# A routed two-layer network on Trainium2: the token list's comparisons and streamed columns laid out by column

## The chip, the cores and the metric

One core of a Trainium2 chip runs the whole program in one launch. The metric is the device time of one execution in microseconds (us); three executions of the kernel before took 3925.69, 3928.92 and 3929.18 us, median 3928.92.

The core's engines work side by side and wait for each other by semaphores: TensorE (PE; its weight loads are shown apart as PEld), VectorE (DVE), ScalarE (ACT), GpSimd (POOL) and the queues that issue transfers (SyncE and GpSimd here). In a matrix product one operand, the stationary one, is loaded as weights, and the columns of the other, the moving one, are streamed past it.

## The reference

```
X   = real(fft(fft(x, axis=1), axis=2))        # x: 8 x 3072 x 256
x   = X as 24576 rows of 256
# routing, capacity 3072 tokens for each of 8 experts, one expert per token
logits = x @ w_gate                            # 24576 x 8
for (token, e) in descending order of logits:
    if token is free and expert e has room: assign it
for e in experts:                              # 256 -> 1024 -> 256
    y[mask_e] = relu(x[mask_e] @ w1[e]) @ w2[e]
h   = y @ w_in                                 # 256 -> 2048
out = (max(h, 0) + alpha * min(h, 0)) @ w_out  # 2048 -> 256, float32
```

The greedy order is computed as eight rounds. In each round the expert that fills next gets its 3072 tokens, and the round's list of those tokens is formed; the list says which rows the expert's tiles gather.

## The kernel before, in words

**Stages.** `fft_phase` computes the transform, writes the rows to memory and leaves the logits in `LG`, token m of column c at partition m, column c (128 partitions, 192 columns). Then `ffn_phase` runs the first round alone, as all else waits for it, and after it 48 tiles of 512 tokens, six for each expert. The other seven rounds run as a generator, `background()`: the tile loop calls it once after each group of products (`l1` to `l4`), before that group's evacuation, and each call emits a small step of a round. Round r begins when tile 6(r − 2) is reached; where a tile's gather needs a list that is not formed yet, the loop draws the rest of the round's steps at once. The order of all instructions is the order in which the program emits them (a manual schedule); each engine takes its own in that order.

**A tile's products.** `l1` (tile `h`), `l2` (`y`), `l3` (`u`) and `l4` (`o`) are products of three parts each, and ScalarE and VectorE evacuate them: `hs`, and for `u` the operations `r`, `a`, `g`.

**A round's list.** `place` ends with `lh`, two 16-bit numbers for each token: its position among the chosen, low seven bits (`lh[:, 0]`) and the rest (`lh[:, 1]`, 0 to 23 for the chosen). The list is a product over partitions: for each of the 192 columns, the stationary operand `ol` (128 x 128) is 1 where a token's low number equals the output partition, and the moving operand `rr` (2 x 24 = 48 columns) holds the partition number and the column number where the token's high number equals the group (`eq`). 192 such products sum into `ls`, which becomes the list `lm` and the row numbers `idx`.

**pack_wide (L607 to L631)** is this for the first round: 24 comparisons on VectorE, one for each group over all 192 columns (L617); two ScalarE products with the partition number `pf` (L618); the products with the column number `colb` on GpSimd and VectorE (L620); then twelve times an `ol` of 16 columns (L625), 16 products (L627) and two dummy products (`warm`, L1028). Ahead of all stand 26 dummy products.

**pack (L633 to L657)** is this for the background rounds, in chunks of 8 columns: `eq` (L644), `ol` (L645) and the two halves of `rr` (L646, L647) on VectorE for two chunks, a pause of two steps (`lag`), then the 16 products (L653). There are 24 chunks in each of seven rounds.

In both, `eq` and `rr` have the group ahead of the column, so that the 48 elements streamed for one column lie apart:

```
rr = wp.tile([P, 2, NG, C], BF16, tag="rr", bufs=2, name="rr")    # pack, C = 8
lv, ol[:, :, j], rr[:, :, :, j]                                   # out, stationary, moving
```

**Beside the first round.** After each step of `pack_wide` the caller places a chunk of the first expert's weights (`place_w`: a ScalarE cast at L814, a GpSimd subtraction at L815) and fetches another (L837, GpSimd's queue). After the list come the gathers of the first rows (L886), 14 dummy products and the first tile.

Of the kernel before, what the change touches and what calls it, by code (L numbers as in the profile page):

```python
# [12 lines left out]
BF16 = mybir.dt.bfloat16  # L13
# [22 lines left out]
def fft_phase(tc, op, x, cWA, cCS, cT, wg, w3, XD, LG, W3S, router):  # L36
    """x -> rows of Re(FFT2) in XD (row = col*128 + m) and gate logits in LG[m, col, e];
    on the side the float64 weights w3 -> float32 halves in W3S."""
    nc = tc.nc
    with ExitStack() as ctx:  # L40
# [11 lines left out]
        def load_x(b, k, n=4):  # L52
            """n of the chunk's four columns, the last of them when part is there."""
            if (b, k) not in xch:
                xch[b, k] = xp.tile([N1, 4, D], F32, tag="x", name=f"x_{b}_{k}")
                o = 0
            else:
                o = 4 - n
            nc.sync.dma_start(
                xch[b, k][:, o : o + n], x[b].rearrange("(a c) d -> a c d", c=N2)[:, 4 * k + o : 4 * k + o + n, :]  # L60
            )
# [8 lines left out]
        # twiddled DFT-32 factors: for the cosine and the sine part, leading bits and rest  # L70
# [4 lines left out]
        def convert():  # L75
            """float64 words -> float32, rounded, as its leading 12 bits and the rest."""
# [13 lines left out]
            for n, (j, q) in enumerate(chunks):  # L90
                load(n + 1)
                raw = raws.pop(n)
                lo, hi = raw[:, :, 0], raw[:, :, 1]
                a = vp.tile([P, CV], I32, tag="a", bufs=1, name=f"a{n}")
                b = vp.tile([P, CV], I32, tag="b", bufs=1, name=f"b{n}")
                V.tensor_scalar(a, hi, 5, 2, op0=ALU.logical_shift_left, op1=ALU.logical_shift_right)
                V.tensor_scalar(b, lo, 28, 1, op0=ALU.logical_shift_right, op1=ALU.bitwise_and)
                yield
                V.scalar_tensor_tensor(a, lo, 29, a, op0=ALU.logical_shift_right, op1=ALU.bitwise_or)
                yield  # L100
                V.scalar_tensor_tensor(a, hi, -(1 << 30), a, op0=ALU.bitwise_and, op1=ALU.bitwise_or)
                yield
                V.tensor_tensor(a, a, b, op=ALU.add)
                # below float32's normal range: zero
                V.tensor_scalar(b, hi, 1, 21, op0=ALU.logical_shift_left, op1=ALU.logical_shift_right)
                yield
                f = b.bitcast(F32)
                V.scalar_tensor_tensor(f, b, 897.0, a.bitcast(F32), op0=ALU.is_ge, op1=ALU.mult)
                yield
                hl = vp.tile([P, 2, CV], F32R, tag="hl", name=f"hl{n}")  # L110
                nc.scalar.copy(hl[:, 0], f)
                yield
                V.tensor_sub(hl[:, 1], f, hl[:, 0].bitcast(F32))
                nc.gpsimd.dma_start(W3S[j, :, :, q * CV : (q + 1) * CV], hl.bitcast(F32))
                yield
# [22 lines left out]
        def load_t(i, after):  # L138
            s = slice(i * TC, (i + 1) * TC)
            # not ahead of the x that is needed first  # L140
            nc.gpsimd.tensor_copy(mark, after)
            nc.gpsimd.dma_start(tw[:, s], cT[:, s])
# [24 lines left out]
        # right-hand factor [C | C wg | S | S wg]  # L167
# [101 lines left out]
class Router:  # L269
    """One round: the expert that fills next in the greedy order, with its TOK/E tokens.  # L270

    The round's threshold is the largest value at which some open expert has CAP tokens that
    rank it first. It is searched bit by bit over ordered integer keys (high 16 bits, then low)."""
# [10 lines left out]
    def lag(self):  # L284
        """Until VectorE, behind TensorE, has done what was asked of it."""
# [4 lines left out]
    def __init__(self, ctx, tc, LG):  # L290
# [17 lines left out]
        # constants of the shapes  # L308
# [10 lines left out]
        with tc.tile_pool(name="r_init", bufs=1) as ip:  # L319
# [18 lines left out]
            # strict prefix sums over partitions and over columns  # L338
# [4 lines left out]
    def open_work(self, ctx, tc):  # L343
        self.wp = wp = ctx.enter_context(tc.tile_pool(name="r_work", bufs=1))
        self.ilo = wp.tile([P, P, self.CH], I16, name="ilo")
        self.ihi = wp.tile([P, NG, self.CH], I16, name="ihi")

    def prep(self, wp, view, n):
        """Best open expert and ordered key of the n columns of a view of [P, NCOL, ...]."""
# [33 lines left out]
    def ordered(self, z0, z1, mx, lo, hi, dn):  # L383
        """Signed integers in the order of the floats mx (-0 as +0): their high half, less for tokens
        done, and their low half less 32768."""
# [13 lines left out]
    def count_wide(self, psum, pool, key, lows, k, at0=None):  # L399
        """Tokens of each expert with key >= each of the last k of lows, less 8 * 1536: [P, E, k] in  # L400
        PSUM, on every partition. With at0, another key and its [P, 1] bound, the first is for that."""
# [31 lines left out]
        # at most 24 * 128 in each: less 1536 exact in 16 bits  # L433
# [10 lines left out]
    def first(self, psum, lists, pool):  # L444
        """The round that all else waits for: four bits a step, in a pool of its own."""
# [3 lines left out]
        # bounds and positions to compare with  # L449
# [8 lines left out]
        nc.gpsimd.iota(self.ihi, pattern=[[1, NG], [0, self.CH]], base=0, channel_multiplier=0)  # L458
# [3 lines left out]
        def search(key, exact=None):  # L462
            """Adds to base the largest 16-bit value at which some expert still has CAP tokens."""
# [33 lines left out]
        # the last step also counts at its base: experts that hold longest, then the first of them  # L497
# [15 lines left out]
    def low_key(self):  # L513
        """Keys relative to the high half found, less 32768, exact near it."""
# [7 lines left out]
    def choose(self, key):  # L522
        """Tokens of the chosen expert above the threshold and at it."""
# [8 lines left out]
    def place(self, psum, lists, at, n, wide=None, ilo=None):  # L532
        """The list of a round, [P, 2, NG]: token m in its column, column; its rows. Then closes
        the expert among n."""
# [4 lines left out]
        # column totals, on 96 partitions each, along 128  # L539
# [28 lines left out]
        # position of the chosen, 30000 for the others  # L568
# [19 lines left out]
        # the tokens are taken; the experts after the closed one move up  # L588
# [18 lines left out]
    def pack_wide(self, pool, lv, lh, ilo):  # L607
        """pack(), all columns of the moving side at once."""
        nc, V = self.nc, self.nc.vector
        C = 16  # L610
        self.warm(26)
        eq = pool.tile([P, NG, NCOL], BF16, tag="ind", name="eq")
        rr = pool.tile([P, 2, NG, NCOL], BF16, tag="rr", name="rr")
        for h in range(2):
            s = slice(h * NG // 2, (h + 1) * NG // 2)
            for g in range(s.start, s.stop):
                V.tensor_scalar(eq[:, g], lh[:, 1], float(g), None, op0=ALU.is_equal)  # L617
            nc.scalar.activation(rr[:, 0, s], eq[:, s], AF.Copy, scale=self.pf)  # L618
        for eng, s in ((nc.gpsimd, slice(0, 8)), (V, slice(8, NG))):
            eng.tensor_tensor(  # L620
                rr[:, 1, s], eq[:, s], self.colb[:, None, :].broadcast_to([P, s.stop - s.start, NCOL]), op=ALU.mult
            )
        for c in range(0, NCOL, C):
            ol = pool.tile([P, P, C], BF16, tag="ol", bufs=2, name="ol")
            V.tensor_tensor(ol, lh[:, 0, None, c : c + C].broadcast_to([P, P, C]), ilo, op=ALU.is_equal)  # L625
            for j in range(C):
                nc.tensor.matmul(  # L627
                    lv, ol[:, :, j], rr[:, :, :, c + j], start=(c + j == 0), stop=(c + j == NCOL - 1)
                )
            self.warm(2)  # L630
            yield  # L631

    def pack(self, lv, lh):  # L633
        """Into lv: the chosen tokens' m and column, each at its position."""
        nc, wp, V = self.nc, self.wp, self.nc.vector
        C = self.CH
        for c2 in range(0, NCOL // C, 2):
            made = []
            for c in (c2, c2 + 1):
                s = slice(c * C, c * C + C)  # L640
                ol = wp.tile([P, P, C], BF16, tag="ol", bufs=2, name="ol")
                eq = wp.tile([P, NG, C], BF16, tag="eq", bufs=2, name="eq")
                rr = wp.tile([P, 2, NG, C], BF16, tag="rr", bufs=2, name="rr")
                V.tensor_tensor(eq, lh[:, 1, None, s].broadcast_to([P, NG, C]), self.ihi, op=ALU.is_equal)  # L644
                V.tensor_tensor(ol, lh[:, 0, None, s].broadcast_to([P, P, C]), self.ilo, op=ALU.is_equal)  # L645
                V.tensor_scalar(rr[:, 0], eq, self.pf, None, op0=ALU.mult)  # L646
                V.tensor_tensor(rr[:, 1], eq, self.colb[:, None, s].broadcast_to([P, NG, C]), op=ALU.mult)  # L647
# [3 lines left out]
            for c, ol, rr in made:  # L651
                for j in range(C):
                    nc.tensor.matmul(  # L653
                        lv, ol[:, :, j], rr[:, :, :, j], start=(c == 0 and j == 0),
# [4 lines left out]
    def rank(self, n):  # L659
        """prep() for the n experts that are left, two bits of the search a step."""  # L660
# [26 lines left out]
    def round(self, psum, lists, n):  # L687
        """A round with n experts left, in small steps beside other work."""
# [15 lines left out]
        def keys(k16):  # L704
            """The key in the row of a token's expert, zero in the others'."""
# [7 lines left out]
        def total(k):  # L713
            """Sums over the partitions of s, [P, n, k], on every one."""
# [44 lines left out]
        # the first expert that holds at the threshold  # L759
# [24 lines left out]
def ffn_phase(tc, XD, wcat, W3S, alpha, out, router):  # L784
    nc = tc.nc
    with ExitStack() as ctx:
# [38 lines left out]
        def expert_idx(r):  # L825
            """Row numbers of the expert's weight chunks, once the round knows the expert."""
# [19 lines left out]
        def out_rows(r):  # L846
            """Rows of out for the tokens of a round."""
# [46 lines left out]
        def transpose_x(t, between=None):  # L894
# [4 lines left out]
            # as the rows come, or one half after the other  # L899
# [124 lines left out]
        def warm(n):  # L1024
            """n products that nothing uses: TensorE's clock falls to half when it stands still."""
# [43 lines left out]
        def background():  # L1069
            """Rounds after the first, each while the expert before it is worked on."""  # L1070
# [71 lines left out]
def _constants():  # L1142
    """Transform matrices; they depend on the shapes alone."""
# [41 lines left out]
def _layout(x, moe_w_gate, moe_w1, moe_w2, moe2_w_in, moe2_w_out, moe2_alpha):  # L1185
    """Permuted copies of the inputs, chunk by chunk as the kernel loads them."""
# [41 lines left out]
```

## Time and profile before

| | us |
|---|---|
| three executions | 3925.69, 3928.92, 3929.18 |
| profiled execution, first to last instruction (its span) | 3928.5 |
| PE busy | 3842.7 (98%) |
| PEld busy | 3376.9 (86%) |
| DVE busy | 2576.7 (66%) |
| ACT busy | 1817.2 (46%) |
| POOL busy | 663.3 (17%) |

The profile is of one execution of its own, whose time is known by its span. Times of single instructions are in nanoseconds. Matrix products are pipelined, so one that is recorded with 275 ns can follow another much sooner, and a busy PE is not one at its peak. The chain of waits follows the work back from the last instruction, at each step to what released it.

### The profile page before, as it was taken

To read this page: it belongs to the slowest core of one execution; us is meant where nothing else is said; L and a number is where in the kernel's file an instruction comes from. 1 tells how busy PE (TensorE), PEld (TensorE's weight loads), DVE (VectorE), ACT (ScalarE), POOL (GpSimd) and SP (SyncE) were. 2 spreads that over 40 slices of the span, in tenths; PEclk is the share of its full clock that TensorE was granted. 3 is DMA by queue.
4 is the path that set the end of the run, shared out by engine and by line. 5 is a ranking of instruction groups with operands and counts; after the bars stand their busy time and mean duration, and the time that the engine had idled before them with its cause. 6 is when DMAs were issued, how large, how long until landed. Compare 5 with 4: busy or idle time off the path is not lost.

```text
span 3928.5 us, 62438 instructions
## 1 busy us (share of the span) xinstructions
PE 3842.7 (98%) x23686; PEld 3376.9 (86%) x23696; DVE 2576.7 (66%) x7667; ACT 1817.2 (46%) x3453; POOL 663.3 (17%) x906
## 2 busy tenths in 40 slices
PE   9999899999999999999999999999999999999999
PEld 9998687888888788888888888888888888888888
DVE  5776799679868976886776776556444444444444
ACT  4553244444444444454444444453455445444454
POOL 2211400030011210030011210030012201111010
PEclk9999899999999999999999999999999999999999
DMA  8786100010000000010000000010001000000000
GB/s 236 199 217 191 44 12 12 10 40 12 12 22 22 22 22 12 12 44 12 12 22 20 25 22 12 12 44 12 12 22 33 22 12 17 28 22 22 12 17 12
DMA packets 95053, 153.53 MB, mean 39 GB/s; under 512 B 14688, under 2 KB 64544, under 8 KB 94752
## 3 DMA queue, kind: packets, MB, share of 16 engines
q0 software_dynamic: 30400, 90.21, 7.5%
q1 hardware_dynamic: 63440, 58.75, 5.3%
q8 instruction: 185, 3.03, 0.3%
q14 instruction: 116, 0.95, 0.1%
q10 hardware_dynamic: 912, 0.58, 0.1%
HBM read 90.77 MB, written 58.72 MB: 38 GB/s over the span
## 4 chain that ended last, share of the span: by engine, by line
PE 83%; DVE 13%; issue 2%; ACT 1%; DMA 1%; POOL 0%; SPq 0%; ACTq 0%; POOLq 0%; DVEq 0%
PE o L992 23%; PE u L912 22%; PE y L912 12%; PE h L912 11%; DVE junk L726 5%; PE b L209 4%; PE ls L653 3%; PE a L150 2%; DVE r L965 2%; PE c L226 2%; DVE g L970 2%; PE xps L902 1%; DMA x<-in_x 1%; PE warm L1028 1%; DVE hs L926 1%
## 5 line engine op out<-in xcount | busy, mean ns | idle before, releaser
L992 PEld LDWEIGHTS o<-w3t,g 128*128 128x128 f32 x9216 | 1177.7, 188 | 91.6 <-DVE g L970 30.0
L992 PE MATMUL o<-w3t,g 128*128 128x256 f32 x9216 | 1208.9, 281 | 26.5 <-DVE g L970 24.3
L912 PE MATMUL u<-ys,w3t 128*128 128x512 f32 x4608 | 1184.9, 394 | 0.2 <-DVE ys L948 0.2
L965 DVE SCALAR_TENSOR_TENSOR r<-a,nal,r 128x512 f32<-128x512 f32 x768 | 597.2, 778 | 657.2 <-ACT a L964 655.5
L912 PEld LDWEIGHTS u<-ys,w3t 128*128 128x128 f32 x4608 | 842.0, 189 | 161.0 <-DVE ys L948 1.2
L963 ACT ACTIVATE r<-u 128x512 f32<-128x512 f32 x768 | 459.7, 599 | 866.1 <-PE u L912 689.9
L1015 POOL DMA_INDIRECT out_dram<-os,orow x192 | 190.4, 992 | 2625.3 <-ACT os L1011 2557.1
L925 ACT ACTIVATE hs<-h 128x512 fp32r<-128x512 f32 x384 | 230.5, 600 | 795.3 <-PE h L912 774.0
L926 DVE SCALAR_TENSOR_TENSOR hs<-h,hs 128x512 fp32r<-128x512 f32 x384 | 264.5, 689 | 408.7 <-ACT hs L925 408.1
L970 DVE TENSOR_TENSOR g<-r,g 128x512 fp32r<-128x512 f32 x768 | 526.8, 686 | 4.3
L912 PE MATMUL y<-hs,wxh 128*128 128x512 f32 x1536 | 490.6, 400 | 0.4 <-DVE hs L926 0.4
L969 ACT CAST g<-r 128x512 fp32r<-128x512 f32 x768 | 478.2, 623 | 22.6 <-DVE r L965 22.6
L964 ACT ACTIVATE a<-u 128x512 f32<-128x512 f32 x768 | 455.0, 592 | 0.0
L726 DVE TENSOR_SCALAR_CACHE_REDUCE junk<-ke 128x192 bf16<-128x192 uint16 x1296 | 367.5, 348 | 0.1
L912 PEld LDWEIGHTS y<-hs,wxh 128*128 128x128 f32 x1536 | 284.3, 189 | 61.6 <-DVE hs L926 1.2
L912 PE MATMUL h<-xth,wxh 128*128 128x512 f32 x768 | 303.9, 396 | 1.9 <-DVE hs L926 1.8
L912 PE MATMUL y<-hs,wxl 128*128 128x512 f32 x768 | 303.6, 395 | 0.0
L912 PE MATMUL h<-xtl,wxh 128*128 128x512 f32 x768 | 301.2, 392 | 0.2 <-DVE xtl L907 0.2
L912 PE MATMUL h<-xth,wxl 128*128 128x512 f32 x768 | 300.2, 391 | 0.0
L886 POOL DMA_INDIRECT xg<-XD,idx x192 | 208.2, 1084 | 83.9 <-issue 55.2
L912 PEld LDWEIGHTS y<-hs,wxl 128*128 128x128 f32 x768 | 144.3, 188 | 35.0
L912 PEld LDWEIGHTS h<-xth,wxl 128*128 128x128 f32 x768 | 144.5, 188 | 32.2
(228 smaller groups left out, 3709.4 us busy)
## 6 DMA issues: line engine op xcount, KB each, us to landing
x<-in_x SPq DMA_DIRECT2D x63, 384.0 KB, 5.0
XD<-xs SPq DMA_DIRECT2D x96, 128.0 KB, 2.7
XD<-xs SPq DMA_DIRECT2D x184, 64.0 KB, 2.6
raw<-in_w POOLq DMA_DIRECT2D x32, 256.0 KB, 4.3
W3S<-hl POOLq DMA_DIRECT2D x32, 256.0 KB, 3.1
w3t<-W3S SPq DMA_DIRECT2D x16, 512.0 KB, 10.2
tw<-in_tw POOLq DMA_DIRECT2D x12, 512.0 KB, 5.9
xg<-XD,idx POOLq DMA_INDIRECT x192, 2.8
```

The source lines that it names most:

```text
L726: V.tensor_scalar(junk[(e + k) % 2], ke[:, e], float((k + 1) * step), 0.0, op0=ALU.is_ge, op1=ALU.add, accum_out=s[:, e, k : k + 1],)
L886: nc.gpsimd.indirect_dma_start(out=x[:, j, :], out_offset=None, in_=XD, in_offset=bass.IndirectOffsetOnAxis(ap=idx[:, j0 + j : j0 + j + 1] ...
L912: nc.tensor.matmul(o, w, a, start=(first and n == 0), stop=(last and n == 2))
L925: nc.scalar.activation(h[:, 0], ps, AF.Relu)
L926: nc.vector.scalar_tensor_tensor(h[:, 1], ps, 0.0, h[:, 0].bitcast(F32), op0=ALU.max, op1=ALU.subtract)
L963: nc.scalar.activation(r, ps, AF.Relu)
L964: nc.scalar.activation(a, ps, AF.Relu, scale=-1.0)
L965: nc.vector.scalar_tensor_tensor(r, a, nal[:, j : j + 1], r, op0=ALU.mult, op1=ALU.add)
L969: nc.scalar.copy(g[:, 0], r)
L970: nc.vector.tensor_sub(g[:, 1], r, g[:, 0].bitcast(F32))
L992: nc.tensor.matmul(o[:, s, :], a, w, start=(j == 0 and n == 0 and s % 2 == 0), stop=(j == 15 and n == 2 and s % 2 == 1), skip_group_check= ...
L1015: ins = nc.gpsimd.indirect_dma_start(out=out, out_offset=bass.IndirectOffsetOnAxis(ap=orow[:, jj : jj + 1], axis=0), in_=os[:, s, :], in_o ...
```

## The change

`eq` and `rr` are laid out by column, so that the 48 elements of one column are contiguous. The constant `ihi` (numbers 0 to 23) is laid out to fit. In `pack` the same four operations are issued for a chunk, on the new shapes. In `pack_wide` the 24 comparisons, the two ScalarE products and the two column products become, for each quarter of 48 columns, one comparison against `ihi`, one ScalarE product and one VectorE product; a quarter's operations stand ahead of its three groups of `ol` and products. GpSimd has no part in it any more. The dummy products ahead are 14 in place of 26, and behind a group one in place of two, except behind the last group of a quarter. Comments and docstrings are gone. Line numbers from L608 on move.

```diff
-        self.ihi = wp.tile([P, NG, self.CH], I16, name="ihi")
+        self.ihi = wp.tile([P, self.CH, NG], I16, name="ihi")
...
-        nc.gpsimd.iota(self.ihi, pattern=[[1, NG], [0, self.CH]], base=0, channel_multiplier=0)
+        nc.gpsimd.iota(self.ihi, pattern=[[0, self.CH], [1, NG]], base=0, channel_multiplier=0)
...
     def pack_wide(self, pool, lv, lh, ilo):
         nc, V = self.nc, self.nc.vector
         C = 16
-        self.warm(26)
-        eq = pool.tile([P, NG, NCOL], BF16, tag="ind", name="eq")
-        rr = pool.tile([P, 2, NG, NCOL], BF16, tag="rr", name="rr")
-        for h in range(2):
-            s = slice(h * NG // 2, (h + 1) * NG // 2)
-            for g in range(s.start, s.stop):
-                V.tensor_scalar(eq[:, g], lh[:, 1], float(g), None, op0=ALU.is_equal)
-            nc.scalar.activation(rr[:, 0, s], eq[:, s], AF.Copy, scale=self.pf)
-        for eng, s in ((nc.gpsimd, slice(0, 8)), (V, slice(8, NG))):
-            eng.tensor_tensor(
-                rr[:, 1, s], eq[:, s], self.colb[:, None, :].broadcast_to([P, s.stop - s.start, NCOL]), op=ALU.mult
-            )
+        self.warm(14)
+
+        eq = pool.tile([P, NCOL, NG], BF16, tag="ind", name="eq")
+        rr = pool.tile([P, NCOL, 2, NG], BF16, tag="rr", name="rr")
+        H = NCOL // 4
         for c in range(0, NCOL, C):
+            if c % H == 0:
+                s = slice(c, c + H)
+                sh = [P, H // self.CH, self.CH, NG]
+                V.tensor_tensor(
+                    eq[:, s].rearrange("p (k c) g -> p k c g", c=self.CH),
+                    lh[:, 1, s].rearrange("p (k c) -> p k c", c=self.CH).unsqueeze(3).broadcast_to(sh),
+                    self.ihi[:, None].broadcast_to(sh), op=ALU.is_equal,
+                )
+                nc.scalar.activation(rr[:, s, 0], eq[:, s], AF.Copy, scale=self.pf)
+                V.tensor_tensor(
+                    rr[:, s, 1], eq[:, s], self.colb[:, s, None].broadcast_to([P, H, NG]), op=ALU.mult
+                )
             ol = pool.tile([P, P, C], BF16, tag="ol", bufs=2, name="ol")
             V.tensor_tensor(ol, lh[:, 0, None, c : c + C].broadcast_to([P, P, C]), ilo, op=ALU.is_equal)
             for j in range(C):
                 nc.tensor.matmul(
-                    lv, ol[:, :, j], rr[:, :, :, c + j], start=(c + j == 0), stop=(c + j == NCOL - 1)
+                    lv, ol[:, :, j], rr[:, c + j], start=(c + j == 0), stop=(c + j == NCOL - 1)
                 )
-            self.warm(2)
+            self.warm(2 if c % H == H - C else 1)
             yield
...
     def pack(self, lv, lh):
...
-                eq = wp.tile([P, NG, C], BF16, tag="eq", bufs=2, name="eq")
-                rr = wp.tile([P, 2, NG, C], BF16, tag="rr", bufs=2, name="rr")
-                V.tensor_tensor(eq, lh[:, 1, None, s].broadcast_to([P, NG, C]), self.ihi, op=ALU.is_equal)
+                eq = wp.tile([P, C, NG], BF16, tag="eq", bufs=2, name="eq")
+                rr = wp.tile([P, C, 2, NG], BF16, tag="rr", bufs=2, name="rr")
+                V.tensor_tensor(eq, lh[:, 1, s, None].broadcast_to([P, C, NG]), self.ihi, op=ALU.is_equal)
                 V.tensor_tensor(ol, lh[:, 0, None, s].broadcast_to([P, P, C]), self.ilo, op=ALU.is_equal)
-                V.tensor_scalar(rr[:, 0], eq, self.pf, None, op0=ALU.mult)
-                V.tensor_tensor(rr[:, 1], eq, self.colb[:, None, s].broadcast_to([P, NG, C]), op=ALU.mult)
+                V.tensor_scalar(rr[:, :, 0], eq, self.pf, None, op0=ALU.mult)
+                V.tensor_tensor(rr[:, :, 1], eq, self.colb[:, s, None].broadcast_to([P, C, NG]), op=ALU.mult)
...
                     nc.tensor.matmul(
-                        lv, ol[:, :, j], rr[:, :, :, j], start=(c == 0 and j == 0),
+                        lv, ol[:, :, j], rr[:, j], start=(c == 0 and j == 0),
```

## Rows read from the trace of the kernel before

**Rows 1.** The page, chain of waits by line, share of the span.

```profile
PE o L992 23%; PE u L912 22%; PE y L912 12%; PE h L912 11%; DVE junk L726 5%; PE b L209 4%; PE ls L653 3%; PE a L150 2%; DVE r L965 2%; PE c L226 2%; DVE g L970 2%; PE xps L902 1%; DMA x<-in_x 1%; PE warm L1028 1%; DVE hs L926 1%
```

**Rows 2.** Chain of waits, first round's list: start us, us, engine, tile, line.

```profile
410.49 7.64 DVE eq L617 x24
418.15 1.76 DVE rr L620
...
421.10 1.71 PE ls L627 x16
422.81 0.85 PE warm L1028 x2
...
446.93 1.70 PE ls L627 x16
```

**Rows 3.** Stages: us, busy us of PE, PEld, DVE, ACT, POOL, clock, DMA share, GB/s.

```profile
408.00:421.00 13.00, 6.62 (x35) 3.11 (x33) 11.94 (x32) 5.69 (x5) 8.06 (x7) 0.89 0.27 81
421.00:449.00 28.00, 27.01 (x212) 21.73 (x217) 16.09 (x14) 1.55 (x3) 13.04 (x8) 0.50 0.14 39
...
2654.00:2756.00 102.00, 102.00 (x678) 90.26 (x677) 62.47 (x145) 39.89 (x74) 8.58 (x12) 1.00 0.04 11
2800.00:2902.00 102.00, 102.00 (x596) 89.83 (x596) 45.10 (x67) 48.41 (x90) 9.19 (x14) 1.00 0.04 13
```

**Rows 4.** Groups by line, PE and PEld: count | busy us, mean ns | idle before.

```profile
L653 PE MATMUL ls<-rr,ol 128*128 128x48 bf16 x1344 | 141.6, 275 | 0.7 <-DVE rr L647 0.7
...
L992 PEld LDWEIGHTS o<-w3t,g 128*128 128x128 f32 x9216 | 1177.7, 188 | 91.6 <-DVE g L970 30.0 <-ACT g L969 3.1 <-issue 1.4
...
L425 PEld LDWEIGHTS <-ind 128*128 128x128 bf16 x24 | 0.9, 98 | 1.0 <-DVE ind L420 1.0
```

**Rows 5.** Timeline, PE and PEld: start us, us from first start to last end.

```profile
402.47 0.29 PEld L425 LDWEIGHTS <-ind 128*128 128x128 bf16 x8 [0.28 <-DVE ind L420]
...
423.46 1.70 PE L627 MATMUL ls<-rr,ol 128*128 128x48 bf16 x16
...
730.88 1.68 PE L653 MATMUL ls<-rr,ol 128*128 128x48 bf16 x16
...
732.29 1.49 PEld L992 LDWEIGHTS o<-w3t,g 128*128 128x128 f32 x12
```

**Rows 6.** Line 653, weight loads: ns min/median/max, first and last start.

```profile
L653 PEld LDWEIGHTS <-ol x1344: 141/146/173, 730.9 to 2754.2; 128*128 128x128 bf16 x192
```

**Rows 7.** Groups by line, VectorE: shapes, count | busy us, mean ns | idle before.

```profile
L645 DVE TENSOR_TENSOR ol<-lh,ilo 128x1024 bf16<-128x1024 int16 x168 | 114.8, 683 | 8.5 <-PE ls L653 8.5
...
L644 DVE TENSOR_TENSOR eq<-lh,ihi 128x192 bf16<-128x192 int16 x168 | 47.5, 282 | 0.1
L646 DVE TENSOR_SCALAR rr<-eq,pf 128x192 bf16<-128x192 bf16 x168 | 45.4, 270 | 0.0
L647 DVE TENSOR_TENSOR rr<-eq,colb 128x192 bf16<-128x192 bf16 x168 | 41.9, 250 | 0.0
...
L625 DVE TENSOR_TENSOR ol<-lh,ilo 128x2048 bf16<-128x2048 int16 x12 | 17.0, 1427 | 8.4 <-PE ls L627 8.4
...
L375 DVE TENSOR_TENSOR oh<-big,aw 128x128 bf16<-128x128 bf16 x11 | 3.1, 282 | 0.0
...
L375 DVE TENSOR_TENSOR big<-big,wE 128x128 bf16<-128x128 bf16 x11 | 2.4, 216 | 0.0
...
L620 DVE TENSOR_TENSOR rr<-eq,colb 128x3072 bf16<-128x3072 bf16 x1 | 1.8, 1759 | 0.0
```

**Rows 8.** Timeline, VectorE in a stretch with a background list.

```profile
2672.52 0.25 DVE L644 TENSOR_TENSOR eq<-lh,ihi 128x192 bf16<-128x192 int16 x1
...
2675.60 0.75 DVE L965 SCALAR_TENSOR_TENSOR r<-a,nal,r 128x512 f32<-128x512 f32 x1 [1.88 <-ACT a L964]
...
2679.28 0.69 DVE L926 SCALAR_TENSOR_TENSOR hs<-h,hs 128x512 fp32r<-128x512 f32 x1 [1.21 <-ACT hs L925]
```

**Rows 9.** Groups by line, ScalarE, first round.

```profile
L618 ACT ACTIVATE rr<-eq,pf 128x2304 bf16<-128x2304 bf16 x2 | 4.4, 2216 | 4.2 <-DVE eq L617 4.2
```

## The prediction

> **What bounds the kernel now.** I read the chain of waits by line first, then stages by window, then the chain inside the first round, then single groups. The chain is TensorE in its largest parts, and the list-building product `ls` alone holds 3% of the span through the background rounds [rows 1]. Two kinds of stage are touched.
>
> In the first round nothing runs beside the list: the chain goes from 24 VectorE comparisons (7.64 us) and one VectorE product (1.76) to the first `ls` product at 421.10, and then through twelve groups of 16 products until 446.93 + 1.70 = 448.63 [rows 2]. VectorE fills 11.94 of the 13 us before 421; from there TensorE fills 27.01 of 28, at a granted clock of 0.50, the lower of its levels of 1.2 and 2.4 GHz [rows 3]. So 10.6 us of preparation are followed by 27.5 us of products, on the path.
>
> In the seven background rounds the list is built beside the feed-forward tiles. In a stretch with such a list TensorE is busy 102.00 of 102 us and VectorE 62.47; in one without, 102.00 and 45.10 [rows 3]. TensorE's 1344 products stood idle 0.7 us in all for the list's own operands [rows 4]. TensorE sets the end there, VectorE has spare time.
>
> **The pace of the list's products.** Sixteen of them take 1.68 us, one 275 ns, so the next starts (1680 − 275)/15 = 94 ns later; in the first round, at half clock, (1700 − 275)/15 = 95 ns [rows 4, 5]. So TensorE's clock does not set it. Either the stationary side does (128 columns, 8 or 16 elements apart: not changed) or the moving side (48 columns, 8 or 192 elements apart: to be made contiguous). Weight loads that follow each other without a pause show which: eight contiguous bf16 loads take 0.29 us, one 98 ns, pace (290 − 98)/7 = 27; twelve f32 loads take 1.49 us, one 188, pace (1490 − 188)/11 = 118 [rows 4, 5]. In both a load's recorded time is 70 ns above its pace. The list's load has a median of 146 [rows 6], so its own pace would be 76, and yet the products come every 94. The 18 ns between are the moving side's, and the change takes them away; then the loads are late next, at 76. The ends of this term: no gain, if the strided loads do need 94; and 94 − 27 = 67 ns, if the strided load got as cheap as the contiguous one. A loss is excluded, since columns and loads stay as many. I take 18, as the only row of the load itself gives it. The sum: 1344 × 18 ns = 24.2 us, all on the path by rows 3; ends 0 and 90.
>
> The Trainium skill, "SBUF — State Buffer", section "Door 1: The DMA port swizzle", says that consecutive accesses within a 16-byte line run at full rate and each step to a new line pays. That fits a pace that the clock does not move. It also speaks against this change: the 128 stationary elements lie on 128 lines, before and after, and at the moving side's 94/48 = 2.0 ns per line (an estimate) they would need 251 ns a load; the 94 ns of rows 5 contradict that. The skill's "TensorE: Matmul & The Clock Gate", section "Weight-path perf modes", gives a way out: full 128-column weights that are not f32 are read as four chunks of 32, packed or strided. No run here shows the chunks. It leads to the second rival.
>
> **VectorE in the background rounds.** Per chunk of 8 columns: `eq` and the column product `rr` get an operand that repeats along the innermost axis. Two bf16 operations of one size show its price: 282 ns with such a repeat (`oh`, 128 elements), 216 without (`big`) [rows 7]. With the 3072 elements of the first round's `rr` in 1759 ns, the plain form costs 149 ns + 0.524 per element, and twice the slope gives 283 for 128, as measured. At 192 elements that is 350 against 250, for each of the two: +0.2 us a chunk; its ends are 0 and, if a whole plain duration were added to each, +0.5. The product with the partition number (270 ns) gets an output of runs of 24 and may keep its time or double its 0.12 us of elements; I take 0. `ol` (683) stays. 24 chunks in 7 rounds: 168 × 0.2 = 34 us of VectorE. It is hidden: after a chunk's four operations VectorE sits idle 1.88 us, then 1.21 us, waiting for ScalarE [rows 8], and 24 × 0.2 = 4.8 us more makes 67 of 102 us busy. Queued behind the longer operations on VectorE are the feed-forward `r`, `g` and `hs`, and TensorE behind those; they move only when the idle time is used up. Without cover it costs the 34 us. I put 0.4 us for the single pair that the first background round needs at once at its end, two chunks at 0.2.
>
> **The first round's list.** Removed: 24 comparisons and VectorE's `rr` (9.4 us on the path), GpSimd's third of `rr`, and the two ScalarE products of 2216 ns [rows 2, 9], which become four of half the size. Added: per quarter an `eq` and an `rr` of 48 × 24 = 1152 elements, both with the repeat: 149 + 1152 × 1.048 = 1356 ns each. Kept: three `ol` a quarter, 1427 ns in the mean, whatever disturbs them included [rows 7]. So VectorE needs 2 × 1.36 + 3 × 1.43 = 7.0 us a quarter, and TensorE 48 × 0.076 + 4 dummy products at 0.43 (half clock, 0.85 for two [rows 2]) = 5.4: VectorE sets the pace. From 410.49 four quarters end at 438.5; one last group of 16 × 0.076 and its drain add 1.5: 440.0 against 448.63, a gain of 8.6 us. Cutting 26 dummy products to 14 costs nothing, since TensorE waits for VectorE there anyway. What follows the list (row gathers, weight splits, tile 0) moves along whole. ScalarE's quarter products now stand between its weight casts, GpSimd's weight fetches behind those: both queues were done long before 440. The ends: 13.4 if the repeat cost nothing here (8 × 0.60 us less); 3.8 if VectorE's `rr` must wait for ScalarE's in the same tile (4 × 1.2, half of a 2216 ns product).
>
> **Sum.** 3928.5 − 24.2 − 8.6 + 0.4 = 3896.1 us. The base is the profiled span; the runs shown have their median 0.4 above it and lie within 3925.69 to 3929.18, so nothing is to be added. Forecast: 3896.
>
> **The rivals.**
> - The weights set the pace already. The loads' steps of 16 and 32 bytes stay, and the pace stays 94. For it: the 70 ns come from contiguous loads, and no row shows them for strided ones. Against: 146 would have to be 164. Only the first round gains, 8.3 us as its last group ends 0.3 later: 3921.
> - The weights cost less than I take. If four weight columns come at once, a load needs 32 steps at the moving side's 94/48 = 2.0 ns: 63 ns, 31 saved, 42 us in place of 24.2: 3878. For it: one price per separate element would explain both sides. Against: 146 − 63 leaves 83 ns beside the pace where two other loads have 70.
> - Slower: VectorE paces the background lists. If the longer bursts push `r` and `g` past the point where TensorE needs them, each chunk's 0.2 us lands on the path, and the faster products only wait: 3928.5 + 34 − 8.6 = 3954. It decides once a chunk adds more than the 1.2 us of idle time behind it. Against: it adds 0.2.
> - The quarters don't overlap: `rr`'s two halves wait for each other across engines, the first round gains 3.8: 3901, inside the forecast's own range.
>
> **How the numbers follow.** Forecast with the fourth rival in it 68%, its own range 3882 to 3909 (12 to 26 ns a product, first round 4 to 12 us); cheaper weights 14%; weights already the limit 12%; slower 6%. The range of 8 in 10 reaches into both neighbours, 3874 to 3922. A measurement of this kernel can tell 0.2%, 7.9 us, from no change. Faster: 68 + 14, and a third of the 12, 86%; the rest of the 12 within it, 8%; slower 6%.
>
> **What would show it.** Right: sixteen `ls` products in about (15 × 76 + 200) = 1.35 us, loads' own time still near 146, VectorE `eq` and `rr` near 350 in the background, no TensorE wait for `r` or `g` in those stretches, the first round's list some 29 us after its first comparison. Wrong: groups still at 1.68 us (the first rival), or VectorE as the releaser of TensorE in the stretches with a list (the third).

## The result and the profile after

The changed kernel took 3885.75 us (median of 4 executions, 3883.63 to 3888.18), the kernel before 3929.05 beside it: a ratio of 0.9889, interval 0.9875 to 0.9903, so 38 to 49 us less. The forecast was 3896, in a range of 3874 to 3922. The profiled execution has a span of 3881.9 us, 46.6 under the span before.

The chain of waits by line, of the page after, answers to [rows 1]: `ls` falls from 3% to 2%, and the large parts keep their order.

```profile
PE o L998 24%; PE u L918 23%; PE y L918 12%; PE h L918 11%; DVE junk L732 5%; PE b L209 4%; PE a L150 3%; DVE r L971 2%; PE ls L659 2%; PE c L226 2%; DVE g L976 2%; PE xps L908 1%; DVE hs L932 1%; DMA x<-in_x 1%; ACT r L969 1%
```

**The background lists.** The groups by line, TensorE's products and loads of the list in the kernel after (count | busy us, mean ns | idle before):

```profile
L659 PE MATMUL ls<-rr,ol 128*128 128x48 bf16 x1344 | 97.4, 220 | 1.8 <-DVE rr L653 1.8
...
L659 PEld LDWEIGHTS <-ol 128*128 128x128 bf16 x1344 | 89.1, 168 | 18.1 <-issue 13.3 <-DVE g L976 3.2 <-DVE ol L651 0.4
```

and three groups in a row on TensorE's timeline after (start us, us):

```profile
1106.18 1.16 PE L659 MATMUL ls<-rr,ol 128*128 128x48 bf16 x16
...
1114.24 1.15 PE L659 MATMUL ls<-rr,ol 128*128 128x48 bf16 x16
...
1122.23 1.16 PE L659 MATMUL ls<-rr,ol 128*128 128x48 bf16 x16
```

The pace is (1150 − 220)/15 = 62 ns, where it was 94 [rows 4, 5]. The two distances add up to 16.05 us, 8.03 each; with the background list of before they were 8.48 (three groups of the run with the first round alone, below). 0.455 us for each of 84 groups is 38.2 us, most of the gain. TensorE is still busy all the time, and VectorE for more of it, in a stretch with a list (the last row of the table by stage, columns as in [rows 3]):

```profile
408.00:421.00 13.00, 6.81 (x63) 4.33 (x61) 12.84 (x11) 5.19 (x7) 11.30 (x9) 0.79 0.37 100
421.00:441.00 20.00, 13.38 (x153) 10.73 (x157) 17.83 (x15) 2.70 (x3) 5.62 (x4) 0.50 0.14 39
2613.00:2707.00 94.00, 94.00 (x658) 82.56 (x657) 65.13 (x142) 39.64 (x74) 9.54 (x12) 1.00 0.04 12
```

65.13 of 94 is 69%, 61% before [rows 3]; 67 of 102, 66%, was forecast. The groups by line of VectorE after show why:

```profile
L650 DVE TENSOR_TENSOR eq<-lh,ihi 128x192 bf16<-128x192 int16 x168 | 64.4, 383 | 0.1
L653 DVE TENSOR_TENSOR rr<-eq,colb 128x192 bf16<-128x192 bf16 x168 | 58.8, 350 | 0.0
L652 DVE TENSOR_SCALAR rr<-eq,pf 128x192 bf16<-128x192 bf16 x168 | 45.6, 271 | 0.0
...
L630 DVE TENSOR_TENSOR ol<-lh,ilo 128x2048 bf16<-128x2048 int16 x12 | 17.2, 1468 | 0.5 <-PE ls L632 0.3
L620 DVE TENSOR_TENSOR eq<-lh,ihi 128x1152 bf16<-128x1152 int16 x4 | 6.5, 1623 | 0.0
L626 DVE TENSOR_TENSOR rr<-eq,colb 128x1152 bf16<-128x1152 bf16 x4 | 6.4, 1594 | 0.1
```

`eq` and the column product cost 101 and 100 ns more each, the partition product nothing [rows 7].

**The first round's list.** The chain of waits after (start us, us):

```profile
408.83 1.37 DVE eq L620
410.23 2.30 DVE rr L626
...
432.65 1.28 DVE eq L620
433.96 1.36 DVE rr L626
...
439.51 0.97 PE ls L632 x16
440.50 0.22 DVE lm L583
```

From the first comparison to the last product it takes 440.48 − 408.83 = 31.7 us, 38.1 before [rows 2]: 6.5 less, 8.6 forecast. VectorE is now the pace, busy 17.83 of the last 20 us while TensorE is busy 13.38. The granted clock is still at its lower level there, 0.50, as before, and the products keep (1190 − 235)/15 = 64 ns all the same (the group at 430.20, shown in the last section). The first group, at 413.72, still ran at a granted clock of 1.00 (stretch 413.70 to 415.00), at (1180 − 220)/15 = 64 ns too; TensorE had then waited 3.31 us for VectorE's `ol`:

```profile
413.72 1.18 PE L632 MATMUL ls<-rr,ol 128*128 128x48 bf16 x16 [3.31 <-DVE ol L630]
```

### The profile page after: what moved, and what is told of

Read it like the earlier page. It is cut to its first block, busy times and chain, and to the rows that moved or that the text cites. A ratio compares the mean times of both kernels' runs of the same rounds, so it can differ in the third digit from the quotient of the medians.

```text
span 3881.9 us, 62378 instructions
## 1 busy us (share of the span) xinstructions
PE 3788.3 (98%) x23666; PEld 3327.8 (86%) x23676; DVE 2611.5 (67%) x7650; ACT 1815.8 (47%) x3455; POOL 657.7 (17%) x905
## 4 chain that ended last, share of the span: by engine, by line
PE 83%; DVE 13%; issue 2%; ACT 1%; DMA 1%; POOL 0%; SPq 0%; ACTq 0%; POOLq 0%; DVEq 0%
PE o L998 24%; PE u L918 23%; PE y L918 12%; PE h L918 11%; DVE junk L732 5%; PE b L209 4%; PE a L150 3%; DVE r L971 2%; PE ls L659 2%; PE c L226 2%; DVE g L976 2%; PE xps L908 1%; DVE hs L932 1%; DMA x<-in_x 1%; ACT r L969 1%
## 5 line engine op out<-in xcount | busy, mean ns | idle before, releaser
L998 PEld LDWEIGHTS o<-w3t,g 128*128 128x128 f32 x9216 | 1178.8, 188 | 92.3 <-DVE g L976 30.7
L998 PE MATMUL o<-w3t,g 128*128 128x256 f32 x9216 | 1209.5, 281 | 27.2 <-DVE g L976 25.2
```

The costliest lines, as they stand in the source:

```text
L998: nc.tensor.matmul(o[:, s, :], a, w, start=(j == 0 and n == 0 and s % 2 == 0), stop=(j == 15 and n == 2 and s % 2 == 1), skip_group_check= ...
```

## The experiments

Three sets ran on chips of their own, each beside the kernel before: 3938.03 us in the first set, 3927.84 in the second, 3929.34 in the third. So ratios are compared, or times of one set.

**What counts: the moving side or the stationary side.** Four runs change one layout each. The first takes the kernel before and lays out its stationary operand alone contiguously:

```diff
-                ol = wp.tile([P, P, C], BF16, tag="ol", bufs=2, name="ol")
+                ol = wp.tile([P, C, P], BF16, tag="ol", bufs=2, name="ol")
...
-                V.tensor_tensor(ol, lh[:, 0, None, s].broadcast_to([P, P, C]), self.ilo, op=ALU.is_equal)
+                V.tensor_tensor(ol, lh[:, 0, s, None].broadcast_to([P, C, P]), self.ilo, op=ALU.is_equal)
...
-                        lv, ol[:, :, j], rr[:, :, :, j], start=(c == 0 and j == 0),
+                        lv, ol[:, j], rr[:, :, :, j], start=(c == 0 and j == 0),
```

> The kernel before, whose background stationary operand alone is laid out contiguously (a step of 1 element in place of 8), the moving side left strided. Theory (the moving side's separate lines set 94 ns): the pace stays at 94 and the time near 3929, unless VectorE, whose comparison for the stationary operand goes from 683 to about 1220 ns, shows. Rival (the strided weights set 94 ns): the pace falls to about 30 ns and the time to about 3845.

It took 3929.38 us, one execution, at a ratio of 0.998. A group on its timeline, and its loads by line:

```profile
1104.33 1.55 PE L653 MATMUL ls<-rr,ol 128*128 128x48 bf16 x16
```

```profile
L653 PEld LDWEIGHTS <-ol 128*128 128x128 bf16 x1344 | 111.0, 114 | 18.3 <-issue 12.8 <-DVE g L970 2.9 <-DVE ol L645 0.7
```

With a product of 264 ns the pace is (1550 − 264)/15 = 86 ns. With contiguous weights the strided moving side alone still takes 86, so the rival, a pace of 30, is out. The 94 that was expected is missed by 8 ns: these came only while both sides were strided. VectorE's `ol` rose to 1220 ns, 90 us more in all, and the time did not rise.

The second takes the run above and brings the moving columns to 8 bytes apart (tiles of 4 columns in place of 8):

```diff
-                rr = wp.tile([P, 2, NG, C], BF16, tag="rr", bufs=2, name="rr")
+                rr = wp.tile([P, C // 4, 2, NG, 4], BF16, tag="rr", bufs=2, name="rr")
...
-                        lv, ol[:, j], rr[:, :, :, j], start=(c == 0 and j == 0),
+                        lv, ol[:, j], rr[:, j // 4, :, :, j % 4], start=(c == 0 and j == 0),
```

> The run with contiguous weights and the old moving side, with one size changed: the moving columns lie 8 bytes apart in place of 16. There the moving side alone set 86 ns for 48 columns, 1.8 ns each. Theory (each 16-byte line costs, not each column): 24 lines, 43 ns, and 84 x 16 x 43 ns = 58 us less than that run's ratio to before (0.998): about 0.983. Rival (any column that is not a neighbour costs 1.8 ns): 86 ns and the same ratio.

3874.62 us, one execution, a ratio of 0.986; a group on its timeline:

```profile
1106.38 0.89 PE L660 MATMUL ls<-rr,ol 128*128 128x48 bf16 x16
```

(890 − 222)/15 = 45 ns, half of 86, for the same 48 columns. So the price goes by the 16-byte lines that the columns touch (24 in place of 48), not by each column that is no neighbour.

The third and fourth take the changed kernel and bring its stationary columns to 8 and to 4 bytes apart (n = 4, n = 2), by a VectorE operation on as many elements:

```diff
-                ol = wp.tile([P, P, C], BF16, tag="ol", bufs=2, name="ol")
+                ol = wp.tile([P, C // n, P, n], BF16, tag="ol", bufs=2, name="ol")
...
-                        lv, ol[:, :, j], rr[:, j], start=(c == 0 and j == 0),
+                        lv, ol[:, j // n, :, j % n], rr[:, j], start=(c == 0 and j == 0),
```

> The changed kernel with one size changed: the background stationary operand's columns lie 4 elements (8 bytes) apart in place of 8 (16 bytes), by the same VectorE operation on as many elements. Theory (weights are late now, and pay for each 16-byte line: half as many lines): the pace falls from 63 to about 32 ns, 84 x 16 x 31 ns = 41 us, 3845. Rival (63 ns is a floor of the product or of any strided load): 63 ns and 3886.

> The changed kernel with the background stationary operand's columns 2 elements (4 bytes) apart in place of 8. With 8 bytes the pace was 34.7 ns. Theory (a load pays for each 16-byte line): a quarter of the lines of the changed kernel, so the pace falls to the product's own floor, 27 to 30 ns as for the contiguous counting products, 84 x 16 x 6 ns = 8 us less than with 8 bytes. Rival (34.7 is already the floor): no difference to 8 bytes. VectorE's operation on runs of 2 elements should keep 685 ns; if not, up to 90 us of VectorE more.

8 bytes: 3854.86 us, a ratio of 0.979 (0.9773 to 0.9807). 4 bytes: 3843.18, 0.9788 (0.9771 to 0.9804), in another set; the two ratios can't be told apart, the paces can. A group on the timeline of each:

```profile
1100.19 0.71 PE L663 MATMUL ls<-rr,ol 128*128 128x48 bf16 x16
```

```profile
1103.26 0.57 PE L663 MATMUL ls<-rr,ol 128*128 128x48 bf16 x16
```

(710 − 192)/15 = 35 ns and (570 − 184)/15 = 26 ns. After the change, then, the weights were late, and they were paid by the line too: 62 ns at 16 bytes, 35 at 8. The 26 at 4 bytes is about the 27 of contiguous loads (the prediction's figure, from [rows 4, 5]), a floor at which the line's price no longer shows. In the first round's list the step is 32 bytes and the pace 64, at the same granted clock of 1.00 too: past 16 bytes it makes no difference. VectorE's `ol` kept 690 ns in both.

**The two parts of the change by themselves.** The changed kernel with the `pack_wide` of before, and with the `pack` of before:

```diff
-        self.warm(14)
...
+        self.warm(26)
...
+            for g in range(s.start, s.stop):
+                V.tensor_scalar(eq[:, g], lh[:, 1], float(g), None, op0=ALU.is_equal)
```

```diff
-                rr = wp.tile([P, C, 2, NG], BF16, tag="rr", bufs=2, name="rr")
+                rr = wp.tile([P, 2, NG, C], BF16, tag="rr", bufs=2, name="rr")
...
-                        lv, ol[:, :, j], rr[:, j], start=(c == 0 and j == 0),
+                        lv, ol[:, :, j], rr[:, :, :, j], start=(c == 0 and j == 0),
```

> The background rounds' list in the new layout, the first round's as before. By the trace of the changed kernel the groups of 16 list products stand 8.04 us apart in place of 8.50, 0.46 us less for each of 84 groups: 38.6 us, so 3929 - 39 = 3890. Rival: much of the gain is the first round's (dummy products and GpSimd out of the way): then over 3900. Groups at a pace near 63 ns either way.

> The first round's list in the new layout, the background rounds' as before. The changed kernel's list took 31.7 us from its first comparison to its last product, in place of 38.1: 6.5 us less, 3922.5. With the background part alone this should add up to the 43 us of the whole; the rival, that the two depend on each other, would miss it by over 5 us. Background groups keep 94 ns and 8.5 us.

The background alone: 3897.43 us beside 3938.03, a ratio of 0.9895 (0.9878 to 0.9911), 35 to 48 us. The first round alone: 3931.68, 0.9985 (0.9975 to 0.9995), 2 to 10 us. Expected were 39 and 6.5. Together they give 47 with an uncertainty of about 10, the whole gave 38 to 49: no sign that one part needs the other. No run takes apart what the first round's part changes at once (layout, quarters, dummy products, GpSimd's share). The first-round kernel's background groups on its timeline, the 8.48 us from above:

```profile
1103.52 1.67 PE L660 MATMUL ls<-rr,ol 128*128 128x48 bf16 x16
...
1111.99 1.68 PE L660 MATMUL ls<-rr,ol 128*128 128x48 bf16 x16
...
1120.48 1.69 PE L660 MATMUL ls<-rr,ol 128*128 128x48 bf16 x16
```

**Is VectorE's part hidden?** The background `eq` and the column product are issued twice:

```diff
                 V.tensor_tensor(eq, lh[:, 1, s, None].broadcast_to([P, C, NG]), self.ihi, op=ALU.is_equal)
+                V.tensor_tensor(eq, lh[:, 1, s, None].broadcast_to([P, C, NG]), self.ihi, op=ALU.is_equal)
...
                 V.tensor_tensor(rr[:, :, 1], eq, self.colb[:, s, None].broadcast_to([P, C, NG]), op=ALU.mult)
+                V.tensor_tensor(rr[:, :, 1], eq, self.colb[:, s, None].broadcast_to([P, C, NG]), op=ALU.mult)
```

> The changed kernel with the background comparison and column product issued twice each: 0.70 us more of VectorE per chunk, 118 us in all, three and a half times what the change itself added. Theory (VectorE's part is hidden behind TensorE, with over 1 us of idle time behind each chunk): within 10 us of the changed kernel. Rival (VectorE's time lands on the path): about 118 us slower, and then some of the change's own 34 us would have landed too.

3895.18 us (ratio 0.992, 0.9904 to 0.9937) beside the changed kernel's 3887.78 in the same set (0.9901, 0.9884 to 0.9917): 7 us at the medians, of 118; the intervals overlap, and at their ends allow 21. TensorE's wait for the list's operands in it, by line:

```profile
L661 PE MATMUL ls<-rr,ol 128*128 128x48 bf16 x1344 | 97.7, 220 | 5.5 <-DVE rr L655 5.5
```

and a stretch with a list, by stage:

```profile
2654.00:2756.00 102.00, 102.00 (x667) 89.64 (x666) 74.41 (x173) 46.83 (x87) 13.06 (x19) 1.00 0.05 15
```

TensorE's wait for `rr` rose from 1.8 to 5.5 us, its wait for the tile `g` from 25.2 to 27.7, which is most of the 7. At the medians over nine tenths stayed hidden.

**Why the first round gained 6.5 and not 8.6.** The timeline after, across engines, at the second quarter:

```profile
416.75 1.42 POOL L821 TENSOR_TENSOR wxl<-rawx,wxh 128x512 fp32r<-128x512 f32 x1
...
416.95 2.44 DVE L620 TENSOR_TENSOR eq<-lh,ihi 128x1152 bf16<-128x1152 int16 x1
```

An `eq` that takes 1.35 us elsewhere takes 2.44 beside a GpSimd subtraction. Five such subtractions fall into the first two quarters. The test puts them on VectorE:

```diff
-        def split_w(dh, dl, raw):
+        def split_w(dh, dl, raw, eng=nc.gpsimd):
             nc.scalar.copy(dh, raw)
-            nc.gpsimd.tensor_sub(dl, raw, dh.bitcast(F32))
+            eng.tensor_sub(dl, raw, dh.bitcast(F32))
...
-                    place_w(0, i)
+                    place_w(0, i, nc.vector)
```

> The changed kernel with the five weight subtractions that run beside the first round's list on VectorE in place of GpSimd. Theory (VectorE stands still while GpSimd subtracts: it lost 4.8 us in the first two quarters): eq and rr fall from a mean of 1.62 and 1.59 to 1.36 us, ol from 1.47 to 1.22, VectorE gains 3.4 us of its own work, the list ends 1 to 3 us earlier and the time falls by as much. Rival (the long ones are due to something else): means as before, and the list 3 us later.

> The changed kernel once more, on the same chip as the others of this set, to compare them with: ratio to the kernel before 0.989, list products 63 ns apart.

3884.15 us, a ratio of 0.9892 (0.9875 to 0.9908), beside 3887.78 of the changed kernel, whose ratio came out at 0.9901 (0.9884 to 0.9917): the times can't be told apart. VectorE's groups by line, first round, can, and they show the cause of the long operations:

```profile
L630 DVE TENSOR_TENSOR ol<-lh,ilo 128x2048 bf16<-128x2048 int16 x12 | 14.4, 1218 | 0.3 <-PE ls L632 0.2
L626 DVE TENSOR_TENSOR rr<-eq,colb 128x1152 bf16<-128x1152 bf16 x4 | 5.4, 1358 | 0.1
L620 DVE TENSOR_TENSOR eq<-lh,ihi 128x1152 bf16<-128x1152 int16 x4 | 5.4, 1350 | 0.0
L821 DVE TENSOR_TENSOR wxl<-rawx,wxh 128x512 fp32r<-128x512 f32 x5 | 3.4, 685 | 1.1 <-ACT wxh L820 1.1
```

17.2 + 6.5 + 6.4 became 14.4 + 5.4 + 5.4: 4.9 us of longer operations gone, 3.4 of subtracting and 1.1 of waiting added. From the last step of `lh` (L577) to the copy of the finished list (L583) it took 30.7 us in place of 32.0, so the list itself gained 1.3.

**A version that beats both.** Stationary steps of 4 bytes in both list forms, and the subtractions on VectorE:

```diff
-            ol = pool.tile([P, P, C], BF16, tag="ol", bufs=2, name="ol")
+            ol = pool.tile([P, C // 2, P, 2], BF16, tag="ol", bufs=2, name="ol")
...
-                    lv, ol[:, :, j], rr[:, c + j], start=(c + j == 0), stop=(c + j == NCOL - 1)
+                    lv, ol[:, j // 2, :, j % 2], rr[:, c + j], start=(c + j == 0), stop=(c + j == NCOL - 1)
...
+                    place_w(0, i, nc.vector)
```

> The kernel with stationary steps of 4 bytes in the background rounds, which ran at 0.9788 of the kernel before, with the same steps in the first round's list and the first round's five weight subtractions on VectorE. In the first round VectorE sets the pace, so the steps gain only in the last group (16 x 36 ns = 0.6 us) and the subtractions 1 to 4 us: 0.978. Rival (the first round's products still cost time): over 5 us less, below 0.9775.

3837.99 us, a ratio of 0.9766 (0.975 to 0.9783): 85 to 98 us under the kernel before, and clear of the changed kernel. Its interval reaches over both expectations, so it isn't shown that it beats steps of 4 bytes in the background alone.

## Why the prediction was right, and where its size was off

**The bound of the stage held.** TensorE's groups set the background stretches, and what the products lost in pace came off the time: 0.455 us a group shorter, 38.2 us over 84 groups; the background alone gave 35 to 48 in the timed runs.

**The moving side was the late one, shown by the run with contiguous weights.** That step of the prediction was right. What failed is the next, "In both a load's recorded time is 70 ns above its pace ... so its own pace would be 76". With the moving side out of the way the loads come every 62 ns, and yet the median recorded load rose after the change,

```profile
L659 PEld LDWEIGHTS <-ol x1344: 140/171/176, 723.7 to 2707.7; 128*128 128x128 bf16 x192
```

from 146 [rows 6] to 171 ns. So a recorded load time is no pace plus a constant: it was 109 ns above its pace here, 71 for the contiguous loads of [rows 4], and 28 in the run where contiguous loads of 114 ns waited for a strided moving side at a pace of 86. The term of 18 ns a product was 31 in truth: by the groups' busy time, (141.6 us/84 − 275 ns)/15 = 94.0 before and (97.4 us/84 − 220 ns)/15 = 62.6 after. A group of 16 has 15 such distances, 471 ns less in all, and 455 of these reached the distance between groups. The sum put 24.2 us where 38.2 came. Per product that is 28 ns, outside the 12 to 26 that the forecast's own range of 3882 to 3909 was made of; the time still fell into that range because it also allowed the first round 12 us, which gave 6.5. That is luck, not insight.

The measured pace is the second rival's 63 to within a nanosecond, and that rival was given 14%. There is luck in this too: its 2.0 ns a line came from the 94 with both sides strided, while the moving side alone pays 86/48 = 1.8, which would make 57. The experiments give the price better: 24 lines fewer saved 41 ns on the moving side, 64 fewer saved 27 ns on the weights, which is 1.7 and 0.42 ns a line, about a quarter. Four weight columns that come at once, as that rival has it, would explain the quarter; no run shows the four themselves. The Trainium skill's rule that each step to a new line pays, weighed in the prediction as speaking against the change ("SBUF — State Buffer", section "Door 1: The DMA port swizzle"), stands: the trace agrees by 86 to 45 ns on the moving side and 62 to 35 on the weights.

**VectorE's price and cover.** Forecast 350 ns for each of two operations, measured 350 and 383; hidden, as forecast, and three and a half times as much on top was nearly hidden too. The rival in which VectorE paces the background lists is out. The one place where VectorE does set the pace is the end of the first background round, where two chunks are drawn at once. The timeline after:

```profile
809.04 1.16 PE L659 MATMUL ls<-rr,ol 128*128 128x48 bf16 x16
...
814.10 0.62 PE L659 MATMUL ls<-rr,ol 128*128 128x48 bf16 x8 [1.01 <-DVE rr L653]
...
815.48 0.62 PE L659 MATMUL ls<-rr,ol 128*128 128x48 bf16 x8 [0.75 <-DVE rr L653]
```

TensorE waits there 1.8 us for `rr`, where [rows 4] had 0.7: 1.1 more, for which the sum had 0.4.

**The first round.** VectorE as its pace and ScalarE's and VectorE's halves side by side: both as forecast. The dummy products ahead are done before TensorE's wait of 3.31 us shown above, so fewer of them cost nothing, as forecast; no run varied them alone. The gain was 6.5 in place of 8.6, as `eq` and `rr` met GpSimd's subtractions too (means of 1.62 and 1.59 us for 1.36), while the sum had let only `ol` meet them. The last rival, quarters that wait for each other, is out: in the second quarter `rr` starts on VectorE and on ScalarE at the same 419.43 (timeline after):

```profile
419.43 1.36 DVE L626 TENSOR_TENSOR rr<-eq,colb 128x1152 bf16<-128x1152 bf16 x1
419.43 1.25 ACT L625 ACTIVATE rr<-eq,pf 128x1152 bf16<-128x1152 bf16 x1 [3.13 <-DVE eq L620]
```

The parts by the trace are 38.2 + 6.5 − 1.1 = 43.6 us, and the medians differ by 43.3. So the total was 10 us better than forecast, for 14 us more from the pace, 2 less from the first round and 0.7 more of waiting for `rr`. Of the 46.6 us by which the spans differ, 1.7 lie before the first comparison (408.83 against 410.49). These need not be the change's: the last step of `lh`, just ahead, starts anywhere from 406.6 to 412.4 in the traces of this case.

## What to carry to other kernels

Where small products follow each other, work out the pace from a group's length, not from what one instruction is recorded with, and ask of both operands how many 16-byte lines they touch. Either side can be cured by bringing neighbours in the streamed order closer together (8 bytes apart on the moving side, 8 or 4 on the stationary side were run here), which leaves the engine that writes the operand its fast, contiguous runs; going all the way to contiguous cost VectorE 90 us for the weights and was not needed. Price a layout's cost on the writing engine at the place where it is used: here the same slower form was all but free beside TensorE and set the pace in the first round.

## What the runs showed of the hardware

- A strided operand's pace does not move with TensorE's clock: 94 and 95 ns at a granted clock of 1.00 and 0.50 before; after, in one and the same list, 64 ns at both (413.72 above and 430.20). At 4 bytes it does: in the first round of the last version the pace is (580 − 183)/15 = 26 ns at a granted clock of 1.00 and (820 − 215)/15 = 40 at 0.50. The timelines of the changed kernel and of the last version:

```profile
430.20 1.19 PE L632 MATMUL ls<-rr,ol 128*128 128x48 bf16 x16 [2.18 <-DVE ol L630]
```

```profile
415.53 0.58 PE L636 MATMUL ls<-rr,ol 128*128 128x48 bf16 x16 [4.06 <-DVE ol L631]
...
417.27 0.82 PE L636 MATMUL ls<-rr,ol 128*128 128x48 bf16 x16 [0.94 <-DVE ol L631]
```

- Two strided operands disturb each other: 86 ns with the moving side strided alone, 94 with both.
- A two-operand VectorE operation loses most of the time in which GpSimd's subtraction runs beside it: `eq` took 2.44 us in place of 1.35, 1.09 more, and it ran beside the subtraction for 1.22 (416.95 to 418.17).
